# GFNet mixing and a snake MLP in one kernel: the first DFT stage of batches 3 to 7 as sums and differences of mirrored rows

## The chip, the cores and the metric

The kernel runs on one core of one Trainium2 chip. The core has a matrix engine (TensorE, PE in the profile; its weight loads are shown apart as PEld), a vector engine (VectorE, DVE), an engine for activation functions (ScalarE, ACT), a programmable one (GpSimd, POOL) and one that here only issues transfers (SyncE, SP). They run beside each other and wait for each other on semaphores. Matrix products are written to PSUM, everything else is kept in SBUF; main memory is reached by DMA, issued here from SP, from POOL and at the start from ACT.

The metric is the device time of one execution in microseconds. Before the change the median of three runs is 786.23 us (786.11 to 787.95).

## The reference: what is computed

The input x has 8 batches of 3008 rows and 256 channels. Each batch is filtered along its rows in the frequency domain, and then every one of the 24064 rows goes through an MLP with the snake activation:

```python
X = np.fft.rfft(x, axis=1)
F = (filt_r + 1j * filt_i)[None, :, :]
y = np.fft.irfft(X * F, n=x.shape[1], axis=1)
...
h = x @ w_in                      # x is y as (24064, 256); w_in is (256, 2048)
s = np.sin(alpha * h)
g = h + s * s / (alpha + 1e-09)
return g @ w_out                  # (2048, 256)
```

All arrays are float32; the kernel computes in float16 with float32 sums.

## The kernel before, in words

**The transform.** 3008 is 47 x 64, so the DFT along the rows is made in two stages. The first (`first`, lines 178 to 187; tiles pa in the profile) is a DFT of length 47 over rows that are 64 apart, for each of the 64 remainders n2. The input is real, so 24 of the 47 frequencies s suffice, each with a real and an imaginary part. A matrix product takes 94 rows of input (47 for a remainder below 32 and 47 for the one 32 above it: the two halves h) and gives 96 rows (2 halves, 24 frequencies, 2 parts); a batch has 16 of them with 512 columns (two remainders of 256 channels). The results are copied from PSUM to the tiles t1_h by `evac` and stored to a scratch buffer d1 in main memory, one store for every four products, on SP's queue.

The second stage reads d1 back in another order (`load_t2`, eight DMAs on POOL's queue, each 192 KB), multiplies with d_t (`forward`, pb), applies the filter on DVE (`product` and `cross`, with a copy of the swapped halves made by DMA, xs), goes back with e_t (`inverse`, pc), through a second scratch buffer d2 (`load_t4`, tiles t4_a, on SP's queue) and ends with a last product (`last`, pd) that leaves y in SBUF.

**The MLP.** The columns of y are cut into 48 chunks of 512 or 384. `hidden` makes one of 16 blocks of 128 hidden units: two products (ph, line 541), a sine on ACT (line 545) and the snake on DVE (line 546, an operation on the sine in SBUF and ph in PSUM; it has the mark "snake"). `project` multiplies back (po, line 558, 16 products of 256 columns for 128 rows), copies to SBUF (line 566) and stores the output, on SP's queue but for the last chunk.

**The order.** It is written out by hand. The main loop has 8 steps for each chunk; a step makes two hidden blocks of chunk k and some projections of chunk k - 1. PE therefore has in a common step 4 ph and 8 po. The spectral work of batches 1 to 7 is put on a list with a due step (`put`); batch b is due around z = 48 b. `slot`, called twice in each step (after the hidden blocks, and after the projections), emits what is due: at most one item with PE work in a slot, unless that is over one step late. Each engine's instructions stay in the order in which they are emitted.

Before the change these are the due steps of a batch from 3 on: x loads z - 92 + 7 ch (four, on POOL's queue), `first` z - 67 + 0.66 i for i from 0 to 15, `load_t2` z - 56, `forward` z - 46.8 + 2.3 u for u from 0 to 11, `inverse` 6 steps later, three of the t4 loads z - 10.5, `last` z - 6.5 + u for the first four and z + 2 u - 9 after. A load of x for batches 2 to 7 is also held (`after`) to the last emitted snake, so that it isn't issued before its step.

`evac` deals copies out in turn, one to DVE and two to ACT. The transfers of SP's queue and of POOL's queue are issued in order, and each queue uses eight semaphores in turn: a DMA waits for the one eight places ahead of it to land. PSUM tiles of the spectral stages come from the pool fps, with two buffers; those of the hidden blocks from hps, with four.

**The tiles.** x and, in batch 0, the filtered products use a pool with four buffers of 8 x 256 columns (`xpool`).

Of the kernel before, what the change touches and what calls it, by code (L numbers as in the profile page):

```python
# [18 lines left out]
B, S, C = 8, 3008, 256  # L19
DFF = 2048  # L20
N1, N2 = 47, 64
NS, NQ = 24, 64
NR = 2 * N1
NK = 4 * NS
FUSED = 1


def dft_tables():

    n1, n2 = np.arange(N1), np.arange(N2)  # L30
    s, q = np.arange(NS), np.arange(NQ)
    ph = 2 * np.pi * np.outer(n1, s) / N1
    w = np.stack([np.cos(ph), -np.sin(ph)], 1)
    wf = np.zeros((N1, 2, 2, NS, 2))
    wi = np.zeros((2, NS, 2, N1, 2))
    v = np.stack([2 * np.cos(ph), -2 * np.sin(ph)], 0)
    v[0, :, 0], v[1, :, 0] = 1.0, 0.0
    for h in range(2):
        wf[:, h, :, :, h] = w
        wi[:, :, h, :, h] = v.transpose(0, 2, 1) * (8.0 / S)  # L40

    kap = np.where(q[:, None] < 32, s + N1 * q[:, None], s + N1 * (95 - q[:, None]))
# [12 lines left out]
    wi0[:, :, :NS] = wi.transpose(0, 2, 1, 3)  # L55
    d = d.reshape(128, NS, 128).astype(f16)
    e = d.transpose(2, 1, 0) * f16(0.125)
    return (wf.reshape(NR, NK).astype(f16), wi.reshape(NK, NR).astype(f16), d,
            wf0.reshape(96, 128).astype(f16), wi0.reshape(128, NR).astype(f16), e)


# [1 line left out]
def kernel(  # L63
# [8 lines left out]
    out: bass.AP,  # L72
):
    nc = tc.nc
    wf_host, wi_host, d_host, wf0_host, wi0_host, e_host = dft_tables()
    wf_dram = nc.inline_tensor(wf_host, name="wf_tbl")
    wi_dram = nc.inline_tensor(wi_host, name="wi_tbl")
    d_dram = nc.inline_tensor(d_host, name="d_tbl")
    wf0_dram = nc.inline_tensor(wf0_host, name="wf0_tbl")
    wi0_dram = nc.inline_tensor(wi0_host, name="wi0_tbl")  # L80
# [6 lines left out]
    def after(ins, other):  # L87

        tc.add_manual_dep(ins.ins, other.ins.name, mybir.DependencyInfo(
            mybir.DependencyClass.Sync, mybir.DependencyReason.DATA), reason="order of loads")  # L90

    def pool(name, bufs, space=None):
        kw = {} if space is None else {"space": space}
        return ctx.enter_context(tc.tile_pool(name=name, bufs=bufs, **kw))

    cpool = pool("consts", 1)
    xpool = pool("xp", 4)
    t2pool = pool("t2", 4)
    xfpool = pool("xf", 3)
    ppool = pool("pp", 4)  # L100
# [4 lines left out]
    dpool = pool("dram", 2, DRAM)  # L105
    fps = pool("fps", 2, PSUM)
# [1 line left out]
    ops = pool("ops", 2, PSUM)  # L108

    wf_t = cpool.tile([NR, NK], FP16)  # L110
    t1_h = [cpool.tile([128, 16, C], FP16, name=f"t1_h{i}") for i in range(2)]
    t4_a = cpool.tile([128, 2, 16, C], FP16)
    t4_h = [t4_a[:, i] for i in range(2)]

    def by_half(t):

        return t.rearrange("p a (b c) -> p (a b) c", c=128)

    cos_all = cpool.tile([128, 4, 512], FP32)
    y = cpool.tile([128, 2, 2, 32, NR], FP16)  # L120
# [4 lines left out]
    for h in range(2):  # L125
        nc.sync.dma_start(out=x32[:, 4 * C * h:4 * C * h + 4 * C],
                          in_=bass.AP(tensor=x.tensor, offset=x.offset + 4 * h * C, ap=[[32 * C, 96], [1, 4 * C]]))
# [8 lines left out]
    marks = {}  # L136

    def load_x(b, ch):
        xt = xpool.tile([NR, 8, C], FP16, name=f"x_{b}_{ch}", tag="x")
        for n0, n in [(0, 8)] if b or ch < 3 else [(0, 4), (4, 4)]:  # L140
            ins = nc.gpsimd.dma_start(  # L141
                out=xt[:, n0:n0 + n],
                in_=bass.AP(tensor=x.tensor, offset=x.offset + (b * S + ch * 8 + n0) * C,
                            ap=[[32 * C, NR], [C, n], [1, C]]),
            )
        if b == 0:
            marks["x", ch] = ins
        if b == 1:
            marks["x1", ch] = ins
            after(ins, marks["w_out"])  # L150
        if b > 1:
            after(ins, marks["snake"])
        return xt
# [3 lines left out]
    def evac(dst, src, on_act=None):  # L157
        flip[0] = (flip[0] + 1) % 3
        if flip[0] if on_act is None else on_act:
            marks["act"] = nc.scalar.copy(out=dst, in_=src)  # L160
        else:
            marks["dve"] = nc.vector.tensor_copy(out=dst, in_=src)  # L162

    class Spectral:

        def __init__(self, b):
            self.b = b
            self.d1 = dpool.tile([2 * NS, N2, C], FP16, name=f"d1_{b}", tag="d1")
            self.d2 = dpool.tile([2 * NS, N2, C], FP16, name=f"d2_{b}", tag="d2")
            self.d1_rows = self.d1.rearrange("a (h n) c -> (a h) n c", h=2)  # L170
            self.d2_rows = self.d2.rearrange("a (h n) c -> (a h) n c", h=2)
            self.x, self.t2, self.t4, self.xf, self.xs, self.p = {}, {}, {}, {}, {}, {}
            self.fused = b >= FUSED

        def load_x(self, ch):
# [2 lines left out]
        def first(self, i):  # L178
            ch, j = divmod(i, 4)
            ps = fps.tile([128, 512], FP32, name=f"pa_{self.b}_{i}", tag="f")  # L180
            marks["pe"] = nc.tensor.matmul(out=ps[0:NK, :], lhsT=wf_t, rhs=self.x[ch][:, 2 * j:2 * j + 2, :],  # L181
                                           start=True, stop=True)
            r0 = 8 * (ch % 2)
            evac(t1_h[ch // 2][0:NK, r0 + 2 * j:r0 + 2 * j + 2, :], ps[0:NK, :])
            if j == 3:
                nc.sync.dma_start(out=self.d1_rows[:, 8 * ch:8 * ch + 8, :], 
                                  in_=t1_h[ch // 2][0:NK, r0:r0 + 8, :])

        def load_t2(self, g):
            self.t2[g] = t2pool.tile([128, 6, C], FP16, name=f"t2_{self.b}_{g}", tag="t2")  # L190
# [73 lines left out]
    id32 = cpool.tile([16, 16], FP32)  # L264
    nc.scalar.dma_start(out=id32, in_=id32_dram.ap())

    x0 = [xpool.tile([NR, 8, C], FP16, name="x_0_0", tag="x")] + [load_x(0, ch) for ch in range(1, 4)]
    nc.gpsimd.dma_start(out=d_t, in_=d_dram.ap())
    id16 = cpool.tile([128, 128], FP16)
    nc.gpsimd.dma_start(out=id16, in_=id16_dram.ap())  # L270
# [25 lines left out]
    for g in range(2):  # L296
        gs = slice(12 * g, 12 * g + 12)
        for k, filt in enumerate((filt_r, filt_i)):
            for q in range(2):
                if (g, k, q) == (0, 1, 1):  # L300
# [3 lines left out]
                    out=f_t[k][64 * k + 32 * q:64 * k + 32 * q + 32, gs, :],  # L304
# [132 lines left out]

    def product_0(i):
        hc, w = blocks[i]
        p0[i] = xpool.tile([128, 2, 4, 128], FP16, name=f"p_0_{i}", tag="x")  # L440
        marks["products"] = nc.vector.tensor_tensor(
            out=p0[i].rearrange("p f s (k c) -> p f s k c", k=2),
            in0=xf0[i].rearrange("p s (k c) -> p s k c", k=2)[:, None].to_broadcast([128, 2, 4, 2, 64]),
            in1=filt_t[:, :, 4 * w:4 * w + 4].rearrange("p f s (k c) -> p f s k c", k=2)[..., 64 * hc:64 * hc + 64],
            op=ALU.mult)
# [24 lines left out]
            after(ins, marks["filt", 1, 0])  # L470
    nc.sync.dma_start(out=wf_t, in_=wf_dram.ap())
    nc.sync.dma_start(out=wi_t, in_=wi_dram.ap())
    w_out32 = vpool.tile([128, 16, C], FP32, name="w_out32", tag="v")
    for jb in range(0, 16, 8):
        ins = nc.sync.dma_start(out=w_out32[:, jb:jb + 8],
# [118 lines left out]
    def put(at, fn, *args, pe=False):  # L594
        pending.append((at, len(pending), pe, fn, args))
# [14 lines left out]
    for b in range(1, B):  # L610
        s = s1 if b == 1 else Spectral(b)
        z = 48 * b
        if b > 1:
            for ch in range(4):
                put((22,27,32,37)[ch] if b == 2 else z - 92 + 7 * ch, s.load_x, ch)
        for i in range(16):
            put(6.9 + 0.35 * i if b == 1 else 36 + 0.66 * i if b == 2 else z - 67 + 0.66 * i, s.first, i, pe=True)
        for g in range(4):
            put(12.5 if b == 1 else max(z - 56, 46.5), s.load_t2, g)
        for u in range(12):  # L620
            inv = 23.5 + 1.25 * u if b == 1 else 59 + 2.1 * u if b == 2 else z - 40.8 + 2.3 * u
            fwd = inv - (6 if b == 1 else 6)
            put(fwd, s.forward, u, pe=True)
            put(fwd + (0.5 if b == 1 else 1.5), s.product, u)
            if s.fused:
                put(fwd + (4 if b == 1 else 4.5), s.cross, u)
            put(inv, s.inverse, u, pe=True)
        for ch in range(4):
            put(z - (9.5 if b == 1 and ch < 3 else (10.5, 10.5, 10.5, 3)[ch]), s.load_t4, ch)
        for u in range(16):  # L630
            put(z + (u - (5 if b == 1 else 6.5) if u < 4 else 2 * u - 9), s.last, u, pe=True)
# [59 lines left out]
```

## Time and profile before

| | us |
|---|---|
| median of 3 runs | 786.23 (786.11 to 787.95) |
| the profiled execution | 785.94 |
| its span, first to last instruction | 784.2 |
| PE busy | 772.0 |
| DVE busy | 656.1 |
| ACT busy | 617.8 |
| POOL busy | 80.0 |

The profile is of one execution, so a sum over its rows is to be set against that execution's own time, 785.94 us, 1.7 more than the span. A row of a group names line, engine, operation, the tile written and the tiles read, the shapes and a count; then the busy time of the group, the mean duration of one instruction in ns, and the engine's idle time just before them. A row of the timeline gives start and duration in us; where it merges several instructions of one line, the count stands at its end (x8), and an idle time before it stands in brackets with what ended it. Matmuls are pipelined, so their durations overlap; the distance from start to start tells what one costs. "SPq" is a transfer issued by SP; a POOL row with DMA is the time in which POOL makes the descriptors, not that of the transfer.

### The profile page before, as it was taken

What the parts mean: (1) busy time and instruction counts of PE and PEld (TensorE: products, weight loads), DVE (VectorE), ACT (ScalarE), POOL (GpSimd) and SP (SyncE); (2) the same over time, 40 slices, a digit from 0 to 9 for tenths busy, and PEclk for the clock granted to TensorE, in tenths of its full rate; (3) what the DMA queues carried; (4) which work ended last, traced back from release to release, by engine and by line L of the source; (5) the groups of instructions that cost most, each with busy time, mean ns of one, the idle gap of its engine ahead of it and who ended that gap; (6) DMA issues with size and microseconds to landing.
All of it is one profiled execution on the core that took longest, in us unless ns stands there. A gap on an engine that the chain in (4) does not pass through costs nothing.

```text
span 784.2 us, 16619 instructions
## 1 busy us (share of the span) xinstructions
PE 772.0 (98%) x5799; PEld 535.1 (68%) x5799; DVE 656.1 (84%) x1169; ACT 617.8 (79%) x1211; POOL 80.0 (10%) x125
## 2 busy tenths in 40 slices
PE   8999999999999999999999999999999999999998
PEld 4757766676667766777667766767667776766666
DVE  7897987899878997799877998799977999777773
ACT  5897988888878887888877887788887887777674
POOL 6342000300020000200020000200002000000000
PEclk9999999999999999999999999999999999999999
DMA  9956667655664546654575454845566243421111
GB/s 218 276 118 159 130 133 221 152 124 121 172 165 89 132 101 190 148 122 107 132 206 111 104 112 132 224 90 117 121 163 174 64 99 81 116 62 28 41 41 54
DMA packets 87692, 100.99 MB, mean 129 GB/s; under 512 B 14488, under 2 KB 75944, under 8 KB 87608
## 3 DMA queue, kind: packets, MB, share of 16 engines
q1 hardware_dynamic: 78032, 73.73, 34.6%
q0 software_dynamic: 9360, 26.15, 17.9%
q8 instruction: 45, 0.74, 0.4%
q14 instruction: 39, 0.32, 0.1%
q10 hardware_dynamic: 216, 0.05, 0.0%
HBM read 55.72 MB, written 46.66 MB: 131 GB/s over the span
## 4 chain that ended last, share of the span: by engine, by line
PE 90%; DMA 4%; DVE 3%; ACT 1%; SPq 1%; issue 1%; POOL 0%; DVEq 0%; ACTq 0%; POOLq 0%
PE po L558 40%; PE ph L541 39%; PE pa L181 3%; PE pd L254 2%; PE pb L201 2%; PE pc L232 2%; DVE v L546 2%; DMA d_t<-d_tbl 1%; DMA filt_t<-in_filt_i_dram 1%; SPq L586 1%; ACT cos_all L545 1%; DMA t_a<-d 0%; PE warm L381 0%; PE pc L453 0%; DMA out_dram<-o 0%
## 5 line engine op out<-in xcount | busy, mean ns | idle before, releaser
L546 DVE SCALAR_TENSOR_TENSOR v<-cos_all,ph 128x512 f16<-128x512 f32 (+1 forms) x768 | 483.2, 672 | 106.4 <-ACT cos_all L545 102.7
L545 ACT ACTIVATE cos_all<-ph 128x512 f32<-128x512 f32 (+1 forms) x768 | 411.1, 591 | 94.4 <-PE ph L541 93.5
L558 PE MATMUL po<-w,v 128*128 128x256 f16 x3008 | 389.5, 273 | 0.0
L541 PE MATMUL ph<-y,w 128*128 128x512 f16 (+1 forms) x1536 | 387.9, 375 | 1.6 <-DVE y L162 0.9
L558 PEld LDWEIGHTS <-v 128*128 128x128 f16 x3008 | 288.2, 98 | 78.4 <-issue 2.1
L541 PEld LDWEIGHTS <-w 128*128 128x128 f16 x1536 | 147.8, 98 | 103.9 <-issue 3.1
L566 ACT COPY o<-po 128x512 f32<-128x512 f32 (+1 forms) x97 | 55.7, 574 | 19.9 <-PE po L558 12.9
L204 ACT CAST xf<-pb 128x512 f16<-128x512 f32 x84 | 50.0, 595 | 13.1 <-PE pb L201 12.3
L193 POOL DMA_DIRECT2D t<-d x56 | 36.4, 670 | 203.2 <-DMA out_dram<-o 121.6
L160 ACT CAST t_h<-pa 96x512 f16<-96x512 f32 x74 | 43.3, 585 | 8.8 <-PE pa L181 8.5
L141 POOL DMA_DIRECT2D x<-in_x_dram x32 | 17.2, 537 | 297.5 <-PE pc L232 160.4
L160 ACT CAST y<-pd 128x376 f16<-128x376 f32 (+1 forms) x82 | 39.4, 480 | 8.8 <-PE pd L254 5.3
L254 PEld LDWEIGHTS <-t_a 96*128 96x128 f16 x448 | 31.3, 97 | 19.0 <-DMA t_a<-d 0.6
L160 ACT CAST g<-pc 128x512 f16<-128x512 f32 x61 | 36.2, 593 | 9.6 <-PE pc L232 9.2
L181 PE MATMUL pa<-x,wf_t 94*96 94x512 f16 x112 | 42.4, 381 | 0.6 <-ACT t_h L160 0.4
L222 DVE TENSOR_TENSOR p<-p,xs 128x512 f16<-128x512 f16 x84 | 35.7, 425 | 2.9
L254 PE MATMUL pd<-wi_t,t_a 96*128 96x94 f16 x448 | 37.2, 204 | 0.3 <-DMA t_a<-d 0.3
L221 DVE TENSOR_TENSOR xs<-xs,filt_t 128x512 f16<-128x512 f16 x84 | 35.2, 419 | 1.5 <-DMA xs<-xf 1.5
L215 DVE TENSOR_TENSOR p<-xf,filt_t 128x512 f16<-128x512 f16 x84 | 35.2, 419 | 0.0
L232 PE MATMUL pc<-p,e_t 128*128 128x256 f16 x168 | 32.1, 273 | 1.3 <-DVE t_h L162 1.3
L201 PE MATMUL pb<-t,d_t 128*128 128x256 f16 x168 | 32.1, 273 | 0.2
L162 DVE CAST y<-pd 128x376 f16<-128x376 f32 (+2 forms) x46 | 24.9, 543 | 1.8 <-PE pd L343 1.0
(66 smaller groups left out, 264.0 us busy)
## 6 DMA issues: line engine op xcount, KB each, us to landing
x<-in_x_dram POOLq DMA_DIRECT2D x30, 376.0 KB, 5.0
d<-t_h SPq DMA_DIRECT2D x28, 384.0 KB
t<-d POOLq DMA_DIRECT2D x56, 192.0 KB, 5.0
xs<-xf SPq DMA_DIRECT2D x168, 64.0 KB
d<-g SPq DMA_DIRECT2D x56, 192.0 KB
t_a<-d SPq DMA_DIRECT2D x28, 384.0 KB
out_dram<-o SPq DMA_DIRECT2D x104, 80.0 KB
w_out<-in_moe_w_out_dram SPq DMA_DIRECT2D x2, 1024.0 KB
```

Of the source, the lines that this page charges most:

```text
L160: marks["act"] = nc.scalar.copy(out=dst, in_=src)
L181: marks["pe"] = nc.tensor.matmul(out=ps[0:NK, :], lhsT=wf_t, rhs=self.x[ch][:, 2 * j:2 * j + 2, :], start=True, stop=True)
L193: nc.gpsimd.dma_start(out=self.t2[g][64 * p:64 * p + 64, :, :], in_=self.d1[a0:a0 + 6, :, :].rearrange("s n c -> n s c"))
L201: nc.tensor.matmul(out=ps[:, i, :], lhsT=d_t[:, s, :], rhs=self.t2[s // 6][:, s % 6, :], start=True, stop=True)
L204: nc.scalar.copy(out=self.xf[u], in_=ps)
L232: nc.tensor.matmul(out=ps[:, i, :], lhsT=e_t[:, 2 * w + i, :], rhs=pt[:, i, :], start=(k == 0), stop=(k == len(pr) - 1))
L254: nc.tensor.matmul(out=psv[:, i, :], rhs=wi_t, start=True, stop=True, lhsT=t4_h[ch // 2][0:NK, n0 % 16 + i, cb * 128:cb * 128 + 128])
L541: nc.tensor.matmul(out=ps[:, 0:n], lhsT=w1[:, cb, jb * 128:jb * 128 + 128], rhs=y_cols[:, cb, c0:c0 + n], start=(cb == 0), stop=(cb == 1))
L545: nc.scalar.activation(out=cs[:, 0:n], in_=ps[:, 0:n], func=AFT.Sin, bias=float(np.pi / 2))
L546: marks["snake"] = nc.vector.scalar_tensor_tensor(out=v[k][:, jb, 0:n], in0=cs[:, 0:n], scalar=-1.0, in1=ps[:, 0:n], op0=ALU.add, op1=ALU. ...
L558: nc.tensor.matmul(out=pso[k][:, t % 2, :], lhsT=v[k][:, jb, 128 * t:128 * t + 128], rhs=w2[:, jb, :], start=(jb == 0), stop=(jb == 15))
L566: nc.scalar.copy(out=o[:, i0:t % 2 + 1, :], in_=pso[k][:, i0:t % 2 + 1, :])
```

## The change

For batches 3 to 7 the first stage is made another way. Row n of the DFT of length 47 and its mirror, row 47 - n, have the same cosine and opposite sines. So the sum of the two rows is multiplied by cosines (24 rows of input, the first alone, and 24 outputs), and the difference by sines. Five remainder classes of 13 remainders each (65 for 64, one is double) fit side by side: 5 x 24 = 120 rows. So a product has 120 rows in and 120 out, one with the table of cosines for the sums and one with that of sines for the differences, for two remainders (512 columns) at a time: 6 pairs with 512 columns and a seventh with 256, 14 products in place of 16.

- The rows are loaded twice in two orders, into `mirror[0]` and `mirror[1]` (`load_mirror`, 14 calls with 15 DMAs per batch on POOL's queue, due z - 92 + 2.6 i + 1.3 k), each held to the last emitted snake. `mirror[1]` is set to zero once before batch 3 (`start_folding`), for the first rows have no mirror.
- `fold` (due z - 65.9 + 1.35 i for i from 0 to 6) makes on GpSimd the sums, into one of four places that are free in other tiles, and then the differences, in place. The sum is held to the last emitted snake.
- `first_folded` (due z - 62.5 + 1.35 i + 0.7 k) makes the two products of a pair. Each has its own copy from PSUM, but for the seventh pair, whose two products share one; 13 copies in place of 16. d1 is stored after the fourth pair and after the seventh, by two DMAs each (cosine and sine parts), in place of four.
- `load_t2` of these batches is due at z - 52 in place of z - 56. `forward` and all later work are where they were.
- The x tiles become slices of one tile `x_all`, and t1_h slices of t1_a, so that the sums can use their free rows; the table of 120 x 2 x 120 is loaded at the start on SP's queue.

```diff
+FOLDED = 3
+NJ, NL = 5, 13
+NF = NJ * NS
...
+    even = np.cos(ph[:NS])
+    odd = -np.sin(ph[:NS])
+    wp = np.einsum("kis,jm->jiksm", np.stack([even, odd]), np.eye(NJ))
+    wp = np.concatenate([wp[:, 1:].reshape(NF - NJ, 2, NF), wp[:, 0].reshape(NJ, 2, NF)])
...
-    t1_h = [cpool.tile([128, 16, C], FP16, name=f"t1_h{i}") for i in range(2)]
+    t1_a = cpool.tile([128, 2, 16, C], FP16)
+    t1_h = [t1_a[:, i] for i in range(2)]
+    wp_t = cpool.tile([NF, 2, NF], FP16)
...
+    x_all = cpool.tile([128, 4, 8, C], FP16)
...
+    STORES = {3: 0, 6: 8}
+    NP = (NL + 1) // 2
+    x_rows = x_all.rearrange("p a n c -> p (a n) c")
+    mirror = [x_rows[:, 16 * k:16 * k + NL, :] for k in range(2)]
+    sums = [t[0:NF, NL:NL + 2, :] for t in (t1_h[0], t1_h[1], x_rows[:, 0:16], x_rows[:, 16:32])]
+
+    def start_folding():
+
+        nc.gpsimd.memset(mirror[1].bitcast(UINT32), 0)
...
+            if self.folded:
+                self.d1_all = dpool.tile([2 * NS, NJ * NL, C], FP16, name=f"d1_{b}", tag="d1f")
+                self.d1 = self.d1_all[:, 1:1 + N2, :]
+                self.d1_fold = self.d1_all.rearrange("(k s) (j l) c -> k (s j) l c", k=2, j=NJ)
...
+        def load_mirror(self, k, l0, n):
+            rows = [mirror[k][0:NF - NJ, l0:l0 + n]] + ([] if k or l0 else [mirror[k][NF - NJ:NF]])
+            for at, t in zip((N2 * (N1 - 1) if k else N2, 0), rows):
+                run = n if at else NL
+                ins = nc.gpsimd.dma_start(
+                    out=t, in_=bass.AP(tensor=x.tensor, offset=x.offset + (self.b * S + at - 1 + l0) * C,
+                                       ap=[[NL * C, NJ], [-N2 * C if k else N2 * C, NS - 1 if at else 1],
+                                           [1, run * C]]))
+                after(ins, marks["snake"])
+
+        def fold(self, i):
+            l0, n = 2 * i, min(2, NL - 2 * i)
+            xa, xb = [t[0:NF, l0:l0 + n, :] for t in mirror]
+            self.e[i] = sums[i % 4]
+            after(nc.gpsimd.tensor_tensor(out=self.e[i][:, 0:n, :], in0=xa, in1=xb, op=ALU.add), marks["snake"])
+            nc.gpsimd.tensor_tensor(out=xa, in0=xa, in1=xb, op=ALU.subtract)
+
+        def first_folded(self, i, k):
+            l0, n = 2 * i, min(2, NL - 2 * i)
+            if n == 2 or k == 0:
+                self.ps1 = fps.tile([128, 2, C], FP32, name=f"pa_{self.b}_{i}_{k}", tag="f")
+            ps = self.ps1
+            if k == 0:
+                src = self.e[i][:, 0:n, :]
+            else:
+                src = mirror[0][0:NF, l0:l0 + n, :]
+            dst = ps[0:NF, 0:2, :] if n == 2 else ps[0:NF, k:k + 1, :]
+            nc.tensor.matmul(out=dst, lhsT=wp_t[:, k, :], rhs=src, start=True, stop=True)
+            if n == 2:
+                evac(t1_a[0:NF, k, l0:l0 + 2, :], ps[0:NF])
+            elif k == 1:
+                evac(t1_a[0:NF, :, l0, :], ps[0:NF])
+            if i in STORES and k == 1:
+                lo = STORES[i]
+                n = l0 + n - lo
+                for part in range(2):
+                    nc.sync.dma_start(out=self.d1_fold[part, :, lo:lo + n, :], in_=t1_a[0:NF, part, lo:lo + n, :])
...
+    nc.sync.dma_start(out=wp_t, in_=wp_dram.ap())
...
+        if s.folded:
+            if b == FOLDED:
+                put(z - 94, start_folding)
+            for i in range(NP):
+                for k in range(2):
+                    put(z - 92 + 2.6 * i + 1.3 * k, s.load_mirror, k, 2 * i, min(2, NL - 2 * i))
+            for i in range(NP):
+                at = z - 62.5 + 1.35 * i
+                put(at - 3.4, s.fold, i)
+                for k in range(2):
+                    put(at + 0.7 * k, s.first_folded, i, k, pe=True)
+        else:
+            if b > 1:
+                for ch in range(4):
+                    put((22, 27, 32, 37)[ch], s.load_x, ch)
+            for i in range(16):
+                put(6.9 + 0.35 * i if b == 1 else 36 + 0.66 * i, s.first, i, pe=True)
         for g in range(4):
-            put(12.5 if b == 1 else max(z - 56, 46.5), s.load_t2, g)
+            put(12.5 if b == 1 else 46.5 if b == 2 else z - 52, s.load_t2, g)
```

More of the change, by code (lines that the diff above doesn't have):

```diff
@@ L57, in dft_tables @@
     e = d.transpose(2, 1, 0) * f16(0.125)
-    return (wf.reshape(NR, NK).astype(f16), wi.reshape(NK, NR).astype(f16), d,
+    even = np.cos(ph[:NS])
+    odd = -np.sin(ph[:NS])
+    wp = np.einsum("kis,jm->jiksm", np.stack([even, odd]), np.eye(NJ))
+    wp = np.concatenate([wp[:, 1:].reshape(NF - NJ, 2, NF), wp[:, 0].reshape(NJ, 2, NF)])
+    return (wp.astype(f16), wf.reshape(NR, NK).astype(f16), wi.reshape(NK, NR).astype(f16), d,
             wf0.reshape(96, 128).astype(f16), wi0.reshape(128, NR).astype(f16), e)
@@ L74 @@
     nc = tc.nc
-    wf_host, wi_host, d_host, wf0_host, wi0_host, e_host = dft_tables()
+    wp_host, wf_host, wi_host, d_host, wf0_host, wi0_host, e_host = dft_tables()
     wf_dram = nc.inline_tensor(wf_host, name="wf_tbl")
     wi_dram = nc.inline_tensor(wi_host, name="wi_tbl")
+    wp_dram = nc.inline_tensor(wp_host, name="wp_tbl")
     d_dram = nc.inline_tensor(d_host, name="d_tbl")
@@ L96 @@
     cpool = pool("consts", 1)
-    xpool = pool("xp", 4)
     t2pool = pool("t2", 4)
@@ L117, in by_half, with x_tile @@
         return t.rearrange("p a (b c) -> p (a b) c", c=128)
+    x_all = cpool.tile([128, 4, 8, C], FP16)
+    x_made = []
+    def x_tile():
+        x_made.append(x_all[:, len(x_made) % 4])
+        return x_made[-1]
     cos_all = cpool.tile([128, 4, 512], FP32)
@@ L138, in load_x @@
     def load_x(b, ch):
-        xt = xpool.tile([NR, 8, C], FP16, name=f"x_{b}_{ch}", tag="x")
+        xt = x_tile()[0:NR]
         for n0, n in [(0, 8)] if b or ch < 3 else [(0, 4), (4, 4)]:
@@ L167, in __init__ @@
             self.b = b
-            self.d1 = dpool.tile([2 * NS, N2, C], FP16, name=f"d1_{b}", tag="d1")
+            self.folded = b >= FOLDED
+            if self.folded:
[3 more added lines that the diff above has]
+            else:
+                self.d1 = dpool.tile([2 * NS, N2, C], FP16, name=f"d1_{b}", tag="d1")
+                self.d1_rows = self.d1.rearrange("a (h n) c -> (a h) n c", h=2)
             self.d2 = dpool.tile([2 * NS, N2, C], FP16, name=f"d2_{b}", tag="d2")
-            self.d1_rows = self.d1.rearrange("a (h n) c -> (a h) n c", h=2)
             self.d2_rows = self.d2.rearrange("a (h n) c -> (a h) n c", h=2)
-            self.x, self.t2, self.t4, self.xf, self.xs, self.p = {}, {}, {}, {}, {}, {}
+            self.e, self.x, self.t2, self.t4, self.xf, self.xs, self.p = {}, {}, {}, {}, {}, {}, {}
             self.fused = b >= FUSED
@@ L265 @@
     nc.scalar.dma_start(out=id32, in_=id32_dram.ap())
-    x0 = [xpool.tile([NR, 8, C], FP16, name="x_0_0", tag="x")] + [load_x(0, ch) for ch in range(1, 4)]
+    x0 = [x_tile()[0:NR]] + [load_x(0, ch) for ch in range(1, 4)]
     nc.gpsimd.dma_start(out=d_t, in_=d_dram.ap())
@@ L439, in product_0 @@
         hc, w = blocks[i]
-        p0[i] = xpool.tile([128, 2, 4, 128], FP16, name=f"p_0_{i}", tag="x")
+        p0[i] = x_tile()[:, 0:4].rearrange("p n (f c) -> p (n f) c", f=2).rearrange("p (f s) c -> p f s c", f=2)
         marks["products"] = nc.vector.tensor_tensor(
@@ L612 @@
         z = 48 * b
[L613 to L617, printed above, removed]
+        if s.folded:
[9 more added lines that the diff above has]
+                    put(at + 0.7 * k, s.first_folded, i, k, pe=True)
+        else:
+            if b > 1:
[3 more added lines that the diff above has]
+                put(6.9 + 0.35 * i if b == 1 else 36 + 0.66 * i, s.first, i, pe=True)
         for g in range(4):
-            put(12.5 if b == 1 else max(z - 56, 46.5), s.load_t2, g)
+            put(12.5 if b == 1 else 46.5 if b == 2 else z - 52, s.load_t2, g)
         for u in range(12):
```

## The prediction

> **What bounds the kernel now.** I read the page from the top: which engine is full, whether its clock is whole, and what the chain that ended last is made of.
>
> ```profile
> span 784.2 us, 16619 instructions
> ...
> PE 772.0 (98%) x5799; PEld 535.1 (68%) x5799; DVE 656.1 (84%) x1169; ACT 617.8 (79%) x1211; POOL 80.0 (10%) x125
> ...
> PEclk9999999999999999999999999999999999999999
> ...
> PE 90%; DMA 4%; DVE 3%; ACT 1%; SPq 1%; issue 1%; POOL 0%; DVEq 0%; ACTq 0%; POOLq 0%
> ```
>
> PE is busy 98% of the span at full clock. A busy PE need not be one at its peak, so the next view is the timeline of PE in a stretch that the change touches (batch 4's first stage):
>
> ```profile
> 285.16 1.04 PE L558 MATMUL po<-w,v 128*128 128x256 f16 x8
> 286.04 1.03 PE L541 MATMUL ph<-y,w 128*128 128x512 f16 x4
> 286.90 0.38 PE L181 MATMUL pa<-x,wf_t 94*96 94x512 f16 x1
> 287.12 1.04 PE L558 MATMUL po<-w,v 128*128 128x256 f16 x8
> ```
>
> Durations overlap (the end of a matmul is modelled), so the price is read from start to start: eight po cost 0.88 us, four ph 0.86, one pa 0.22. No idle time is printed in any row. Windows over the first stages of batches 4, 5 and 6 say the same:
>
> ```profile
> 284.08:307.43 23.35, 23.30 (x155) 15.13 (x153) 19.40 (x35) 18.59 (x37) 0.00 (x0) 1.00 0.53 150
> 375.76:398.82 23.06, 23.06 (x155) 15.14 (x152) 19.61 (x35) 18.63 (x37) 0.00 (x0) 1.00 0.51 142
> 470.78:493.84 23.06, 23.06 (x154) 15.13 (x152) 19.41 (x35) 18.56 (x36) 0.00 (x0) 1.00 0.54 154
> ```
>
> The columns after the length are PE, weight load, DVE, ACT and POOL busy. PE is full, DVE is at 84%, ACT at 80%, POOL is empty. So in these stages a matmul taken away is worth its spacing, and any wait put on PE costs its length.
>
> **The change, part by part.** All sums are against the profiled execution, 785.94 us (span 784.2); the median of the runs shown, 786.23, lies 0.29 above it.
>
> *Products.* Per batch 16 pa of 512 columns become 12 of 512 and 2 of 256. At 0.22 us for a pa, and 0.109 for 256 columns (the po spacing): 16 x 0.22 = 3.52 before, 12 x 0.22 + 2 x 0.11 = 2.86 after, 0.66 less. Five batches: 3.3 us off PE, all of it on the path. 120 rows and columns instead of 94 and 96 change nothing I can see: ph with 128x128 has a spacing of 0.216.
>
> *Evacuations.* 16 copies of 512 columns become 13 (0.58 us on ACT, 0.68 on DVE each). Neither engine is the bound; worth nothing in time.
>
> *The sums and differences on POOL.* 14 operations per batch, 12 of 120x512 and 2 of 120x256, f16 in and out. The trace has no f16 one; the nearest rows are the weight products on POOL:
>
> ```profile
> L482 POOL TENSOR_TENSOR w<-w_in,y 128x512 f16<-128x512 f32 x2 | 2.5, 1274 | 0.0
> L285 POOL TENSOR_TENSOR rest<-al,part 16x128 f32<-16x128 f32 x1 | 0.4, 419 | 0.1
> ```
>
> I take 1.28 us, and 0.1 for the semaphore between the sum and the difference (the idle time in the second row): 1.38. Bounds: 0.42, which DVE needs for the same shape (its L221 rows), and 1.9, POOL's mean for 128x1024 (L514). Does PE wait? Sum i is released by the last snake (L546) of the step where it was put, about 1.7 us after that step's last ph made way for the next matmul (in the timeline the step starting at 288.29 is through its ph at 289.15, its second snake ends at 290.9). I counted the matmul work between release and use in the new order of PE, at the spacings above. Counted from the first release (batch 4), sum 0 is due after 4.8 us and difference 0 after 6.8; the sixth operation after 12.0, the tenth after 17.9, the twelfth after 19.8, the fourteenth (half size) after 22.7. Twelve operations in a row take 12 x 1.38 = 16.6, but the release of sum 5 comes only at 13.7, so operation 12 ends at 13.7 + 2.8 = 16.5: 3.3 us to spare, the least of all. PE waits only if an operation takes over 19.8 / 12 = 1.65 us. So nothing at my value; at 1.9 it is 12 x 1.9 - 19.8 = 3.0 us late per batch, 15 in all. I lean on the 1274 row since shape, operation and output type are the same.
>
> *The hold on the snake.* Queued behind a held sum on POOL are only the other sums, the next t2 loads (put 5.8 steps after the last sum) and the later mirror loads; nobody else waits for POOL. Cost nothing.
>
> *Sharing with DVE.* While POOL multiplied weights, DVE's snakes ran beside it:
>
> ```profile
> 36.79 1.84 POOL L482 TENSOR_TENSOR w<-w_in,y 128x768 f16<-128x768 f32 x1
> ...
> 39.13 1.85 POOL L482 TENSOR_TENSOR w<-w_in,y 128x768 f16<-128x768 f32 x1
> ```
>
> ```profile
> 37.55 4.87 DVE L546 SCALAR_TENSOR_TENSOR v<-cos_all,ph 128x512 f16<-128x512 f32 x8 [1.10 <-ACT cos_all L545]
> ```
>
> Eight snakes in 4.87 us are 0.61 each, and pairs later, with POOL idle, take 1.28, the same; POOL's 1.84 is also what it takes before the snakes start. So snakes and POOL do not slow each other. What that stretch does not show is DVE's f16 products (0.42 us, two SBUF inputs) beside POOL. In the new order of DVE only one or two crosses of the batch before (two products each) fall among the sums. Bounds: nothing, or each of up to four products delayed by one POOL operation, 1.28 us, a pair back to back by 2.6; a snake's result is needed by the ph four buffers later, some 2 us of slack, so at most 0.6 us per pair, 3 to 6 us in all. I take nothing. The Trainium skill, "SBUF — State Buffer", section "Who interferes with whom", says that a DVE instruction with two SBUF inputs and a GpSimd instruction that reads SBUF exclude each other for a whole instruction; the snake has one SBUF input, which fits the row above, and by that rule the crosses would cost up to those few us. The same skill's "GPSIMD Engine Reference", section 4.1, advises against elementwise work on GpSimd since VectorE is about twice as fast; here DVE is at 84% in these stages and POOL at 0, so the trace speaks for the slower engine.
>
> *Loads.* Instead of 4 x loads, 15 mirror loads per batch (0.54 us of POOL each, 8 us where it is idle), about the same bytes in smaller pieces, landing (5 us) over ten steps before the sums. Nothing; nor do one memset on idle POOL and one 58 KB table load on SP's queue at the start, where the chain runs through other loads (d_t, filters).
>
> *The handoff to the second stage.* This is the tight place. The last pa moves from step z-57 to z-53.5, the t2 load from z-56 to z-52, while the first pb stays at z-46. Batch 4 before:
>
> ```profile
> 306.33 0.38 PE L181 MATMUL pa<-x,wf_t 94*96 94x512 f16 x1
> ...
> 323.24 0.38 PE L201 MATMUL pb<-t,d_t 128*128 128x256 f16 x2
> ```
>
> ```profile
> 302.84 0.32 SPq L186 DMA_DIRECT2D d<-t_h  x1
> 303.25 1.62 SPq L244 DMA_DIRECT2D t_a<-d  x3
> 307.73 0.30 SPq L186 DMA_DIRECT2D d<-t_h  x1
> ```
>
> ```profile
> 313.37 3.28 POOL L193 DMA_DIRECT2D t<-d  x5 [33.00 <-DMA out_dram<-o]
> ```
>
> Last pa 306.33, store issued 307.73, landed and t2 issued 313.37, its second half issued 0.65 later and landed at 317.8: 11.5 us, and pb came 5.4 later. The other batches take 11.6, 11.2, 10.9 and 11.2. After the change the matmuls between last pa and pb are 28 ph, 20 pd (0.041) and 48 po in batches 4 and 6, where 20 of the ph have 384 columns (0.162): 3.2 + 1.7 + 0.8 + 5.2 = 11.0 us; in 3, 5 and 7, with 56 po and full ph, 13.0. So 4 and 6 have between -0.6 and +0.1 us left, 3, 5 and 7 at least 1.4. Against it: the last rows go in two stores (0.35 more on SP), 614 KB instead of 393, 0.9 us at the 250 GB/s of these rows' DMA, and in 3, 5 and 7 a store shares its semaphore with a store of the first eight rows, so it waits for that landing, up to 1.5 us. For it: the t4 loads and the first store no longer precede it as closely (DMA share 0.86 over 303.5 to 312.5), and the last evacuation comes after the step's snakes, about 1.1 to 1.4 us after pa instead of 1.4 to 2.3. Bounds: never late, or late by 1.8 in 4 and 6 and by 0.5 in the others, 5.1 in all. I take 0.3 in batches 4 and 6: 0.6.
>
> Sum: 785.94 - 3.3 + 0.6 = 783.2 for a profiled execution, 783.5 for the median.
>
> **The rivals.** *The handoff is late* (1 to 5.1 us in all): 783.9 to 788.0, which reads as no change. For it: the margin of about nothing in two batches. Against it: 1.4 us or more in three.
>
> *POOL becomes the pace* (slower). Place: operations 8 to 14 of each batch. It decides from 1.65 us per operation; the gain is gone when five batches wait 0.66 each, at 1.65 + 0.66 / 12 = 1.70; at 1.9 us the median is 786.2 - 3.3 + 15 = 798, at 1.8 (1.8 us late per batch) 792. Against it: the 1274 row; for it: f16 operands and the crosses are unmeasured there.
>
> *PE does not get the time*: if the steps were paced by DVE or ACT, 786.2. The windows above, with PE at 23.06 of 23.06, speak against it.
>
> **How the numbers follow.** A measurement of this kernel can tell about 0.3%, 2.4 us, from no change: faster is below 783.9, slower above 788.6. The forecast (783.5, itself 782.5 to 783.9) gets 0.52; the late handoff and the unmoved bound 0.26, both "same"; POOL as pace, or a port shared with DVE, 0.22, from 788.6 up. The range begins at 782.4, the full gain of 3.3 with half a us of spread, and ends at 790, a part of the last case; about 0.15 stays outside above.
>
> **What would show it.** Right: 70 products of the new line, 60 of them at 0.22 us spacing; PE's list of waits with under 2 us on the new products and pb; POOL rows of about 1.28 us; steps of the fold stretch as long as their matmuls. The handoff shows as PE pb waiting for a DMA in batches 4 and 6. Wrong: POOL rows over 1.65 us and PE waiting for POOL in the second half of each stage; snakes above 0.61 from start to start; or DVE products above 0.42.

## The result and the profile after

The change made the kernel slower: 791.2 us median (six runs, 790.75 to 793.01) against 786.4 for the kernel before on the same chip, a ratio of 1.0063 [1.0052, 1.0074]. The forecast was 783.5, the range 782.4 to 790; the time lies above both. The profiled execution took 790.9 us with a span of 789.1, which is 4.9 more than the span before.

The first lines of the page after, in the order of those shown of before:

```profile
span 789.1 us, 16812 instructions
...
PE 769.5 (98%) x5789; PEld 532.8 (68%) x5789; DVE 660.6 (84%) x1164; ACT 613.2 (78%) x1201; POOL 195.0 (25%) x251
...
PEclk9999999999999999999999999999999999999999
...
PE 87%; DVE 8%; DMA 2%; ACT 2%; issue 1%; SPq 0%; ACTq 0%; DVEq 0%
```

PE is busy 2.5 us less, at the same clock, in a span 4.9 us longer. So the products did get cheaper, and PE now stands idle where it did not before. In the chain that ended last DVE's share went from 3% to 8%. PE's list of waits (total, times, longest) names the place in its first line; the two lines under it, and the shorter ones that follow, have their like, within some tenths of a us, in the list of before, whose first two lines stand below (the same program lines have other numbers there):

```profile
PE pc L303 <- DVE p L293: 6.8, 7, 1.4
PE warm L452 <- DVE idle L381: 1.5, 1, 1.5
PE pc L303 <- DVE t_a L179: 1.5, 1, 1.5
```

```profile
PE warm L381 <- DVE idle L310: 1.5, 1, 1.5
PE pc L232 <- DVE t_h L162: 1.3, 1, 1.3
```

The waiting matmul is pc, the first product of the inverse transform, which the change does not touch. It waits for the last product of the cross in front of it, on DVE. The groups of instructions (busy, mean ns of one, idle before) show that product and its partner longer than before. First the groups after, then the two of before:

```profile
L293 DVE TENSOR_TENSOR p<-p,xs 128x512 f16<-128x512 f16 x84 | 40.7, 484 | 2.9
L303 PE MATMUL pc<-p,e_t 128*128 128x256 f16 x168 | 32.2, 273 | 8.3 <-DVE p L293 6.8
L292 DVE TENSOR_TENSOR xs<-xs,filt_t 128x512 f16<-128x512 f16 x84 | 38.1, 453 | 2.2 <-DMA xs<-xf 2.2
```

```profile
L222 DVE TENSOR_TENSOR p<-p,xs 128x512 f16<-128x512 f16 x84 | 35.7, 425 | 2.9
L221 DVE TENSOR_TENSOR xs<-xs,filt_t 128x512 f16<-128x512 f16 x84 | 35.2, 419 | 1.5 <-DMA xs<-xf 1.5
```

A mean over 84 hides it: nearly all still take 0.42, a few take three times that. The timeline of DVE after, at the start of batch 4's first stage (start, duration, what), shows one such pair between snakes:

```profile
290.24 1.27 DVE L618 SCALAR_TENSOR_TENSOR v<-cos_all,ph 128x512 f16<-128x512 f32 x2
291.43 1.04 DVE L292 TENSOR_TENSOR xs<-xs,filt_t 128x512 f16<-128x512 f16 x1
292.50 1.26 DVE L293 TENSOR_TENSOR p<-p,xs 128x512 f16<-128x512 f16 x1
293.68 1.27 DVE L618 SCALAR_TENSOR_TENSOR v<-cos_all,ph 128x512 f16<-128x512 f32 x2
```

POOL in the same microseconds has the first sums of the batch:

```profile
289.81 1.14 POOL L236 TENSOR_TENSOR t_a<-x_all 120x512 f16<-120x512 f16 x1 [16.75 <-DVE v L618]
291.03 1.16 POOL L237 TENSOR_TENSOR x_all<-x_all 120x512 f16<-120x512 f16 x1
292.14 1.33 POOL L236 TENSOR_TENSOR t_a<-x_all 120x512 f16<-120x512 f16 x1
293.56 1.22 POOL L237 TENSOR_TENSOR x_all<-x_all 120x512 f16<-120x512 f16 x1
```

And PE:

```profile
290.61 1.03 PE L613 MATMUL ph<-y,w 128*128 128x512 f16 x4
291.47 1.04 PE L630 MATMUL po<-w,v 128*128 128x256 f16 x8
293.82 0.39 PE L303 MATMUL pc<-p,e_t 128*128 128x256 f16 x2 [1.31 <-DVE p L293]
```

The POOL operation of 291.03 ends at 292.19, and xs, begun at 291.43, ends 0.28 later at 292.47; the next POOL operation ends at 293.47, and p ends 0.29 later at 293.76. Each product ends as if most of it had been held until POOL was through. The pair takes 2.33 us from the start of xs to the end of p, where it took 0.87. The matmul that reads p starts at 293.82, 1.47 us after the po before it gave way (291.47 + 0.88); the bracket prints 0.16 less, since the row's end is modelled. The snakes on both sides have their old duration.

The same place before, DVE and then PE:

```profile
291.41 0.41 DVE L221 TENSOR_TENSOR xs<-xs,filt_t 128x512 f16<-128x512 f16 x1
291.85 0.43 DVE L222 TENSOR_TENSOR p<-p,xs 128x512 f16<-128x512 f16 x1
```

```profile
291.54 0.38 PE L181 MATMUL pa<-x,wf_t 94*96 94x512 f16 x1
291.76 1.04 PE L558 MATMUL po<-w,v 128*128 128x256 f16 x8
292.63 0.38 PE L181 MATMUL pa<-x,wf_t 94*96 94x512 f16 x1
292.85 1.03 PE L541 MATMUL ph<-y,w 128*128 128x512 f16 x4
293.71 0.38 PE L232 MATMUL pc<-p,e_t 128*128 128x256 f16 x2
```

Before, p was ready at 292.28 and pc came at 293.71: 1.4 us of slack. A slot takes at most one item with PE work, and the pa took the slots around the cross, so that two pa and four ph (0.22 + 0.22 + 0.86 us) stood in front of pc that are not there after. The change moves the first pa to later steps, pc moves up to right behind the cross, and the slack is gone: a p of the old length would have ended at 292.30 (291.43 + 0.87), and the po gave way at 292.35. So two things meet there: the cross got 1.46 us longer, and nothing is left in front of its reader to hide it.

The balance of the two spans: products 3.3 us less; 1.47 more at the last cross before each of batches 4 to 7, 5.9 together; 0.97 and 0.54 at the two crosses before batch 3's stage; 0.5 at one inverse of batch 5 (at 464.11 us), where no product is stretched but DVE had waited 0.85 us for the xs of the cross before. That is +4.6 against the +4.9 measured.

### The profile page after: what moved, and what is told of

Read it like the earlier page. It is cut to its first block, busy times and chain, and to the rows that moved or that the text cites. A ratio compares the mean times of both kernels' runs of the same rounds, so it can differ in the third digit from the quotient of the medians.

```text
span 789.1 us, 16812 instructions
## 1 busy us (share of the span) xinstructions
PE 769.5 (98%) x5789; PEld 532.8 (68%) x5789; DVE 660.6 (84%) x1164; ACT 613.2 (78%) x1201; POOL 195.0 (25%) x251
## 4 chain that ended last, share of the span: by engine, by line
PE 87%; DVE 8%; DMA 2%; ACT 2%; issue 1%; SPq 0%; ACTq 0%; DVEq 0%
PE po L630 38%; PE ph L613 37%; DVE v L618 4%; PE pd L325 2%; PE pb L272 2%; PE pc L303 2%; PE pa L249 2%; DVE p L293 1%; DMA xs<-xf 1%; DVE xs L292 1%; ACT cos_all L617 1%; PE pa L214 1%; PE pc L524 1%; PE warm L452 1%; DMA cos_all<-in_x_dram 1%
## 5 line engine op out<-in xcount | busy, mean ns | idle before, releaser
L226 POOL DMA_DIRECT2D x_all<-in_x_dram x75 | 47.5, 635 | 159.9 <-DVE v L618 159.3
L177 ACT CAST t_a<-pa 120x512 f16<-120x512 f32 (+1 forms) x66 | 39.0, 591 | 10.3 <-PE pa L249 7.5
L236 POOL TENSOR_TENSOR t_a<-x_all 120x512 f16<-120x512 f16 x20 | 23.9, 1196 | 90.1 <-DVE v L618 88.2
L293 DVE TENSOR_TENSOR p<-p,xs 128x512 f16<-128x512 f16 x84 | 40.7, 484 | 2.9
L292 DVE TENSOR_TENSOR xs<-xs,filt_t 128x512 f16<-128x512 f16 x84 | 38.1, 453 | 2.2 <-DMA xs<-xf 2.2
L237 POOL TENSOR_TENSOR x_all<-x_all 120x512 f16<-120x512 f16 (+1 forms) x35 | 38.4, 1096 | 2.7
```

What stands on the lines that cost most here:

```text
L226: ins = nc.gpsimd.dma_start(out=t, in_=bass.AP(tensor=x.tensor, offset=x.offset + (self.b * S + at - 1 + l0) * C, ap=[[NL * C, NJ], [-N2 * ...
L292: nc.vector.tensor_tensor(out=xs, in0=xs, in1=f_t[1][:, 2 * u:2 * u + 2, :], op=ALU.mult)
L293: nc.vector.tensor_tensor(out=p, in0=p, in1=xs, op=ALU.add)
```

## The experiments

All ratios are to the kernel before on the same chip, with a 95% interval where one was measured.

### Take the meeting away in batches 4 to 7

The first theory is that the meeting of the cross with the sums is the whole loss. Its test lets the first sum of each of these batches wait for that cross instead of a snake, one step later where needed:

```diff
-            after(nc.gpsimd.tensor_tensor(out=self.e[i][:, 0:n, :], ..., op=ALU.add), marks["snake"])
+            after(nc.gpsimd.tensor_tensor(out=self.e[i][:, 0:n, :], ..., op=ALU.add),
+                  marks["cross" if i == 0 and self.b > FOLDED else "snake"])
...
-            nc.vector.tensor_tensor(out=p, in0=p, in1=xs, op=ALU.add)
+            marks["cross"] = nc.vector.tensor_tensor(out=p, in0=p, in1=xs, op=ALU.add)
...
-                put(at - 3.4, s.fold, i)
+                put(max(at - 3.4, z - 64.9) if b > FOLDED else at - 3.4, s.fold, i)
```

> The changed kernel, but in batches 4 to 7 the first sum waits for the last cross of the batch before instead of for its step's snake, and is put 1 step later; batch 3 is as it was. Theory (DVE's products and POOL's sums hold each other up): in batches 4 to 7 the last xs and p products are back at 0.42 and 0.43 us, the four waits of pc for DVE of 1.3 us in the list (1.47 beyond the spacing) are gone, POOL still keeps ahead of PE, and the time falls by 4 x 1.47 = 5.9 from 791.2 to 785.3. First rival (pc waits because PE reaches it earlier now that the products pa have left those steps, and POOL has no part): the waits stay, 791. Second rival (the sums come too late now): PE waits for POOL at the first product of each batch.

Measured: 786.33 us, ratio 0.9997 [0.9984, 1.0011]. A later run of the same kernel, beside the change itself and with more runs:

> The kernel with the first sum of batches 4 to 7 behind the last cross once more. Theory: 5.9 less than the change on the same chip, ratio 0.9985 to 0.999; its first runs gave 0.9997 with an interval of 0.0014 to each side.

It gave 785.02, ratio 0.9982 [0.9973, 0.9992], and its trace shows the pair at its old length, with the POOL operation behind it (DVE, then POOL):

```profile
291.50 0.42 DVE L293 TENSOR_TENSOR xs<-xs,filt_t 128x512 f16<-128x512 f16 x1
291.96 0.42 DVE L294 TENSOR_TENSOR p<-p,xs 128x512 f16<-128x512 f16 x1
```

```profile
292.47 1.15 POOL L236 TENSOR_TENSOR t_a<-x_all 120x512 f16<-120x512 f16 x1 [19.34 <-DVE p L294]
```

Of PE's waits for p this is left, the two at batch 3, whose sums this edit leaves alone:

```profile
PE pc L304 <- DVE p L294: 1.2, 2, 0.8
```

So the four waits went, and with them 4.9 and 6.3 us of time (791.2 to 786.33, and 791.35 to 785.02), where four times 1.47 are 5.9.

### Take it away in all five batches

The same for batch 3 too (the edit is shown against the one above); the last cross of batch 2 is put 1.1 steps earlier, to stand where those of the later batches do:

```diff
-                  marks["cross" if i == 0 and self.b > FOLDED else "snake"])
+                  marks["cross" if i == 0 else "snake"])
...
-                put(max(at - 3.4, z - 64.9) if b > FOLDED else at - 3.4, s.fold, i)
+                put(max(at - 3.4, z - (64.9 if b > FOLDED else 64.4)), s.fold, i)
...
-                put(fwd + (4 if b == 1 else 4.5), s.cross, u)
+                put(fwd + (4 if b == 1 else 3.4 if (b, u) == (2, 11) else 4.5), s.cross, u)
```

> As the run with the first sum behind the last cross, now for batch 3 too, with the last cross of batch 2 put 1.1 steps earlier so that it stands where those of the later batches do. Theory: no product of DVE is stretched after the first 60 us, no wait of pc for DVE at a batch's sums, POOL still ahead of PE: 1.5 us less than that run's profiled 785.6, so 783.6 to 784.2 profiled, a median of 784 to 785, ratio 0.997 to 0.999. Rival (pc waits anyway because the products pa have left): waits of about 0.5 to 1 us at batch 3 stay and the ratio is 1.000.

Measured: 784.64 us, ratio 0.9968 [0.9956, 0.998]. Again, in the company of the change:

> The kernel with all first sums behind the last cross once more. Theory: 1.5 less than the run before it on the same chip, ratio 0.997.

Measured: 783.6 us, ratio 0.9969 [0.9955, 0.9984]. The view of one line (count, then duration in ns as least, median, greatest) of p in this kernel, and then in the changed one:

```profile
L294 DVE TENSOR_TENSOR p<-p,xs x84: 424/425/426, 80.6 to 661.6; 128x512 f16<-128x512 f16 x84
```

```profile
L293 DVE TENSOR_TENSOR p<-p,xs x84: 424/425/1264, 80.0 to 669.0; 128x512 f16<-128x512 f16 x84
```

No product is stretched any more, and no pc waits for p in its list of PE's waits. In the first of the two runs one pc still does, for 0.70 us; there too nothing is stretched, but DVE had waited 1.27 us for the xs of the cross before. Both runs are 0.3% faster than the kernel before, about what the forecast of 783.5 had given. The control on that chip was the change once more:

> The changed kernel once more, beside the next two on one chip: ratio 1.006, PE waiting for p at pc in each batch.

It took 791.35, ratio 1.0055 [1.0042, 1.0069], with the same waits.

### Leave the meeting, give pc its slack back

Here the sums stay where the change has them, and only the last inverse of the batch before goes one step later:

```diff
-                put(inv, s.inverse, u, pe=True)
+                put(inv + (1 if u == 11 and b >= FOLDED else 0), s.inverse, u, pe=True)
```

> The changed kernel, but the last inverse of batches 3 to 7 is due one step later (about 2 us); POOL and DVE are as they were. Theory (the products are stretched to 1.04 and 1.26 us, and that is paid only because pc stands right behind them): both durations stay, the waits of pc in batches 4 to 7 are gone, 785.3. Rival (DVE as a whole falls behind, pc is only where it is seen first): another wait of about the same length takes its place, at ph for a snake or at pc again, and the time stays at 790 to 791.

Measured: 786.67 us, ratio 1.0002 [0.9991, 1.0013]. DVE and PE at the same place:

```profile
291.80 1.05 DVE L292 TENSOR_TENSOR xs<-xs,filt_t 128x512 f16<-128x512 f16 x1
292.88 1.26 DVE L293 TENSOR_TENSOR p<-p,xs 128x512 f16<-128x512 f16 x1
```

```profile
293.58 1.04 PE L630 MATMUL po<-w,v 128*128 128x256 f16 x8
294.45 0.38 PE L303 MATMUL pc<-p,e_t 128*128 128x256 f16 x2
```

The products are as long as in the change, p ends at 294.14, and pc comes at 294.45 without a wait. A stretched product alone costs PE next to nothing when its reader has slack; 4.5 us came back (791.2 to 786.67). The time does not fall to 783, as the 3.3 us of the products alone would give: this trace still has batch 3's waits (1.5), small ones of ph and of the first pa behind the late snakes (about 0.3 us per batch), and 0.73 of pb in batch 4.

### Add the sums to the kernel before

The reverse: the kernel before, with 14 sums and differences per batch on POOL, at the steps and with the hold of the change, on a small tile that nobody reads. Its output stays that of the kernel before.

```diff
+    extra = parts_a.rearrange("p a b -> p (a b)").bitcast(FP16)
...
+    def beside(i):
+
+        a = extra[0:120, 0:512 if i < 6 else 256]
+        after(nc.gpsimd.tensor_tensor(out=a, in0=a, in1=a, op=ALU.add), marks["snake"])
+        nc.gpsimd.tensor_tensor(out=a, in0=a, in1=a, op=ALU.subtract)
...
+                put(z - 65.9 + 1.35 * i, beside, i)
```

> The kernel before, plus the 14 sums and differences per batch on POOL at the steps and with the holds of the change, on a small tile that nobody reads. Theory: the last xs and p of the batch before are stretched as in the changed kernel (about 1.0 and 1.26 us), 1.45 in sum; but here pa products still stand between them and pc, which came 1.4 us after the cross, so PE waits 0.1 to 0.2 per batch and the time is 786.4 to 787.5. First rival (the stretch is paid whatever stands between): 786.4 + 4 x 1.47 + 1.5 = 793.8. Second rival (POOL's sums alone don't stretch them, the change's other traffic does): products at 0.42, 786.4.

Measured: 788.5 us, ratio 1.0024 [1.0014, 1.0034]. The pair on DVE at batch 5's stage, and PE behind it:

```profile
384.81 1.05 DVE L221 TENSOR_TENSOR xs<-xs,filt_t 128x512 f16<-128x512 f16 x1
385.89 1.15 DVE L222 TENSOR_TENSOR p<-p,xs 128x512 f16<-128x512 f16 x1
```

```profile
385.82 0.38 PE L181 MATMUL pa<-x,wf_t 94*96 94x512 f16 x1
386.04 1.03 PE L543 MATMUL ph<-y,w 128*128 128x512 f16 x4
387.09 0.39 PE L232 MATMUL pc<-p,e_t 128*128 128x256 f16 x2
```

The products are stretched here too, without any of the change's products, loads or stores; but a pa stands in front of pc, and PE loses 0.18 us at this place and nothing at batches 4, 6 and 7, where the stretch is smaller (p alone at 4 and 7, xs at 0.76 and p at 1.15 us at 6). The rival's 793.8 is refuted. The time lies a us above what the theory gave; 1.08 and 0.14 at batch 3 are seen as waits of pc, the rest is not attributed.

The same with memsets in place of sums (four per pair, about 0.53 us each), which write that tile and read nothing:

```diff
-        after(nc.gpsimd.tensor_tensor(out=a, in0=a, in1=a, op=ALU.add), marks["snake"])
-        nc.gpsimd.tensor_tensor(out=a, in0=a, in1=a, op=ALU.subtract)
+        after(nc.gpsimd.memset(a, 0.0), marks["snake"])
+        for _ in range(3):
+            nc.gpsimd.memset(a, 0.0)
```

> As the run before, with two memsets on POOL in place of each sum or difference: POOL is as busy at the same places, but reads nothing from SBUF. Theory, that it is POOL's reading that shuts out a product with two SBUF inputs: the products stay at 0.42 and 0.43 us, 786.4. Rival, that any work on POOL does it: stretched as with the sums. The Trainium skill, SBUF — State Buffer, section Who interferes with whom, states the first.

One run: 786.46 us. POOL, and the pair on DVE beside it:

```profile
290.44 1.69 POOL L613 MEMSET parts_a<- 120x512 f16 x3
292.19 0.53 POOL L611 MEMSET parts_a<- 120x512 f16 x1
```

```profile
291.93 0.41 DVE L221 TENSOR_TENSOR xs<-xs,filt_t 128x512 f16<-128x512 f16 x1
292.38 0.42 DVE L222 TENSOR_TENSOR p<-p,xs 128x512 f16<-128x512 f16 x1
```

POOL is busy through both products and neither is longer. None of the 84 pairs of this run is longer than 0.43 us a product. So it is not that POOL is busy; what the two runs differ in is that the sums read their data from SBUF and the memsets only write. The Trainium skill, "SBUF — State Buffer", section "Who interferes with whom", says just this: a DVE instruction with two SBUF inputs and a GpSimd instruction that reads SBUF hold each other out for a whole instruction, and one that only writes does not. These two runs agree, at 0.76 to 1.15 us for a product that meets a sum, against 0.42 beside memsets.

### Is it the hold?

A rival put the loss on the hold, which lines the sums up with the end of a snake, where a cross starts. Its test lets the sums go whenever their rows have landed:

```diff
-            after(nc.gpsimd.tensor_tensor(out=self.e[i][:, 0:n, :], ..., op=ALU.add), marks["snake"])
+            nc.gpsimd.tensor_tensor(out=self.e[i][:, 0:n, :], ..., op=ALU.add)
```

> The changed kernel without the hold of the sums to their step's snake (the loads keep theirs). The sums 0 to 3 then run as soon as their rows have landed, some 8 steps before the held ones, and meet crosses 8 to 10 of the batch before; sums 4 to 6 wait for a free place until the first products. Theory: products are stretched there in place of the last cross, and PE waits about 1.4 us for each one with a pc right behind it: 1 to 3 per batch, 788 to 800 in all; PE never waits for POOL. Rival (it is the hold, which lines the sums up with the end of a snake and so with the crosses, that makes them meet): few are met by chance, 783 to 786.

One run: 800.58 us. PE's waits for p nearly double:

```profile
PE pc L303 <- DVE p L293: 12.6, 9, 3.9
```

Unheld, the first four sums and differences run some eight steps earlier, among more crosses, and 24 products are stretched, up to 1.89 us. The time rose by 9.4 us and this line by 5.8; the rest of this one run is not attributed. The hold does not cause the meetings; it limits them to one or two per batch.

### More meetings on purpose

If each meeting in front of a pc without slack costs about 1.5 us, sums that cover two crosses must cost more. A first attempt put all sums 2.3 steps earlier:

```diff
-                put(at - 3.4, s.fold, i)
+                put(at - 5.7, s.fold, i)
```

> The changed kernel with the sums put 2.3 steps (one cross) earlier, hold as it is. Theory: they meet the crosses 10 and 11 of the batch before, four stretched products per batch in place of two, and PE waits about 1.4 us for each pair: 791.2 + 4 x 1.4 = 796.8, within 1.5. Rival (only the last pc has no slack): 791. Second rival (the sums were late for PE, and more lead helps): below 791.

It took 840.9 us and is no test of this: so early, the fifth sum overwrites the place of the first before the product that reads it, so this kernel computes something else from these rows, and its largest wait is a different one:

```profile
PE pa L249 <- POOL t_a L236: 26.9, 10, 3.3
```

The expectation had overlooked the reuse of the four places. The second attempt moves only the first three pairs:

```diff
-                put(at - 3.4, s.fold, i)
+                put(at - (5.7 if i < 3 else 3.4), s.fold, i)
```

> The changed kernel with the first three pairs of sums and differences put 2.3 steps (the distance of two crosses) earlier, the other four as they are. Theory: in batches 4 to 7 the products of the crosses 10 and 11 meet them, four stretched products per batch in place of two, each pair with a pc right behind it: 4 x 1.4 = 5.6 more than the change, 796 to 797, ratio 1.012 to 1.014. Rival (only the last pc of a batch lacks slack, or the sums were late): as the change, ratio 1.006, or less.

Measured: 792.57 us, ratio 1.0077 [1.0062, 1.0092], beside 1.0055 [1.0042, 1.0069] for the change on the same chip. The direction is as the theory had it, the size is not. DVE in batch 4:

```profile
289.67 1.05 DVE L292 TENSOR_TENSOR xs<-xs,filt_t 128x512 f16<-128x512 f16 x1
290.76 1.26 DVE L293 TENSOR_TENSOR p<-p,xs 128x512 f16<-128x512 f16 x1
...
294.93 1.04 DVE L292 TENSOR_TENSOR xs<-xs,filt_t 128x512 f16<-128x512 f16 x1
296.00 0.43 DVE L293 TENSOR_TENSOR p<-p,xs 128x512 f16<-128x512 f16 x1
```

The first cross meets two POOL operations and PE loses 1.39 to 1.57 there; the second meets one only, xs alone is stretched, and PE loses 0.70 to 0.72. That is 8.7 us in four batches where the change has 5.9, 2.8 more; the expectation had priced two full pairs. Elsewhere this trace has less: one wait at batch 3 in place of two, and no wait behind a late xs, which cost the change's run on this chip 0.87. So PE's waits for p, as listed, are 8.4 us against 7.2 there, 1.2 more, and the medians differ by 1.2 too. The two profiled spans differ by 3.5, which these waits explain only in part.

## Why the prediction was wrong

*Sharing with DVE: "I take nothing".* This is the step that failed, and with it the sign. It had the right mechanism on the table, with bounds of nothing to "3 to 6 us in all", and chose the lower end although no row spoke for it: the rows shown there were snakes, which have one SBUF input, and the products at issue have two. A product does lose a POOL operation, as the upper bound had it: in batches 4 to 7, 0.42 became 1.04 to 1.15 for xs and 1.26 for p, and "DVE products above 0.42" was among its signs of being wrong. The bound went wrong in the reader. It followed a snake to "the ph four buffers later, some 2 us of slack", and took off that slack. The reader that decides is the pc right behind the cross, whose slack was not looked up. In the trace of before it is 1.4 us, and the change itself takes it away, since the pa that held pc back leave these slots. So the price per batch is 1.47, not "at most 0.6", and with batch 3's 1.5 it is 7.4 us in all: 1.4 above the upper bound. With this, 0.1 for the handoff and the 0.5 behind a late xs the prediction's own sum gives 785.94 - 3.3 + 8.0 = 790.6, against 790.9 in the profiled execution. The experiments show both halves by themselves: no meeting (783.6 to 784.6), or the meeting with the slack back (786.7).

*Rivals.* The 0.22 for "slower" held "a port shared with DVE", priced only from 788.6 up and not worked out; what happened is that case. POOL did not become the pace, and PE would get the time: the version without the meetings gives it.

*Products: right.* New products start 0.220 us apart for 512 columns and 0.113 for 256, 0.65 us less per batch. The version without meetings lands at 783.6 and 784.6, where the forecast said 783.5; that is another kernel than the one forecast, so it speaks for this term and not for the sum.

*Sums on POOL: right, a little high.* 1.155 us is typical for 120x512 in place of 1.28, 1.33 when it meets a product, 0.669 for 256 columns. PE never waited for POOL in the change.

*Loads: right in time.* A mirror load costs POOL 0.635 us in place of 0.54, and POOL's busy time went from 80 to 195 us; no wait follows.

*Handoff: mis-sized, 0.6 taken and about 0.1 found.* Last pa to t2 landed takes 10.8, 11.2, 10.8, 10.2 and 12.7 us in batches 3 to 7 and leaves margins of 2.35, 0.14, 2.37, 0.98 and 0.47. Batch 4 was tight as said (its first pb starts 0.13 us after the po before it gave way), batch 7 more than thought. The lost 1.47 lies ahead of the last pa, so it does not widen these margins.

## What to carry to other kernels

Before elementwise work goes to an idle POOL, list the DVE instructions with two SBUF inputs that will run beside it, and for each look up in the trace who reads its result and how long that reader could still wait. When a change moves filler work, that work may have been somebody's slack: follow the readers in the new order, not in the old. Here holding the first sum of each batch behind the last such product (and putting one cross of batch 2 earlier) turned 0.6% slower into 0.3% faster.

## What was unexpected of the hardware

A DVE product of two SBUF tiles (128x512 f16, 0.42 us) that meets a sum on POOL ends 0.27 to 0.30 us after the POOL operation does, however early it began: 0.78 to 1.26 us in the change. Two products in a row meet two POOL operations, since POOL's next one begins before the first product has ended (292.14 against 292.47 above). The POOL operation is held back too, 1.33 us for 1.155. With POOL only writing (memsets), both products stay at 0.42; two snakes, which have one input in PSUM, take 1.27 us beside the sums and 1.28 in the kernel before.

Open: xs landed late at one cross of batch 5 in some executions, and the next pc waited (0.5 us in the change, 0.87 in its second run and in one run of the version without meetings, nothing in the other). The trace of the kernel before has no such wait there. Whether the change has a part in it is open; no run was made on that.
